# A sliding-window attention with a gated layer behind it: one written list gives the order of every engine

## The chip, the core and the metric

The kernel runs on one core of one Trainium2 chip. The metric is the device time of one execution in microseconds (us), taken as the median of several runs. The engines are TensorE (PE, with its weight loads PEld), VectorE (DVE), ScalarE (ACT), GpSimd (POOL) and SyncE (SP). SP, ACT and POOL can issue DMA transfers.

## The reference

There are 8 batches of 8 heads with 576 positions and 64 columns. The attention sees the last 128 positions only and has a linear bias for each head; its result, 4608 tokens of 512 columns, goes through two matrices with a gate between them.

```
scores = q @ k.T / sqrt(64) + slope[head] * -|i - j|      # where 0 <= i - j < 128, else -1e9
attn   = softmax(scores);  x = (attn @ v), heads side by side: [4608, 512]
h = x @ w_in                      # [4608, 2048]
g = h * sigmoid(beta * h)
out = g @ w_out                   # [4608, 512]
```

Inputs and outputs are fp32; the kernel works in bf16 with sums in fp32.

## The kernel before

**Attention.** Tokens of a batch are taken in blocks of 128 (the fifth has 64). q, k and v are loaded in fp32 (`get`, `get_pair`, L200 to L222; tile `fst`, 14 buffers) by SP, cast to bf16 (`cast_qk`, `cast_pair`, `cast_v`, tile `bst`, 4 buffers, or straight into `VS`), and q and k are turned so that the 64 columns lie on partitions (`QK`). For batches 0 and 1 a step `TP` does this on PE, one pair of heads at a time, with one copy by DVE for k and one by ACT for q (L289, L293); for later batches a transposing DMA of SP does it (`DT`, L409). From batch 3 on, v comes by a casting DMA that POOL issues (`get_v`).

Scores of two heads come into two PSUM banks, computed by matmuls on 64 rows, two at a time (`SP_` for batches 0 and 1, in a part A and a part B; `SC`, L438, for the others, m = 0 or 1). ACT takes exp of them (tile `pt`), DVE multiplies by the decay and mask (`factor`, L171 and L176), PE multiplies by v with a column of ones (`PVP`, `PV`, `PVB`), DVE divides by the sum (`norm`, L358 and L359, L499 and L500), and the result is turned into `XT` (features on partitions, a ring of 1536 tokens): on PE with a copy for batches up to 3 (`XP`, `X`), by a transposing DMA of SP later. The last 64 rows of batches 0 and 1 go their own way (`TT`, `SCT`, `PV`).

**The gated layer.** Nine groups of 512 tokens. For each group 16 hidden tiles (`Hm`, L557: four matmuls of 512 columns, then tanh by ACT into `sig`, L564, then one DVE operation into `gT`, L565, which makes h * (1 + tanh(beta h / 2))) and four output tiles (`OS`, L588: 16 matmuls in four steps, then a copy with the factor 0.5 by ACT into `osb`, L598, 5 buffers, then a store). `W1` and `W2` come in four pieces of 512 KB each (in bf16) by casting DMAs that POOL issues.

**Order.** PE, SP and POOL run in the order in which the program calls the steps (a manual schedule); for the first steps ACT and DVE do so too, later a scheduler places them. The calls are made by hand for the first 16 hidden tiles and by a spreading function afterwards (`spread`): it lays the attention steps of later batches (`att`) between hidden and output steps in proportion to their weights. In one call, a step does its matmuls and also the work of ACT and DVE on them. PSUM is handed out by pools (`psum_t`, `psum_h`, `psum_x`, later `psum_o` and `psum_s`) with names for their uses: `SS`, `ST` and `SX` for scores, `hps`, `hpo`, `ops` and `oph` for hidden and output tiles. The last output tile is made in two column halves of 256, which share a bank (L588 to L599).

Dummy matmuls on zeros (`idle`, `calm`) keep PE busy while it waits at the start.

Of the kernel before, what the change touches and what calls it, by code (L numbers as in the profile page):

```python
# [15 lines left out]
P = 128  # L16


@with_exitstack
def kernel(  # L20
# [18 lines left out]
    NQB = 5  # L39
# [44 lines left out]
    psum_c = ctx.enter_context(tc.tile_pool(name="psum_c", bufs=1, space=bass.MemoryType.PSUM))  # L84
    psum_h = ctx.enter_context(tc.tile_pool(name="psum_h", bufs=2, space=bass.MemoryType.PSUM))
    trans = ExitStack()
    psum_t = trans.enter_context(tc.tile_pool(side="right", name="psum_t", bufs=2, space=bass.MemoryType.PSUM))
    SS = psum_c.tile([P, 2, 512], F32, name="SS")
    psum_c.seal()
    opening = ExitStack()  # L90
    psum_x = opening.enter_context(tc.tile_pool(name="psum_x", bufs=1, space=bass.MemoryType.PSUM))
    SX = psum_x.tile([P, 2, 512], F32, name="SX")
    late, gates = {"tick": 0}, {}
    spans = [SS]

    def span():

        spans.append(spans.pop(0))
        return spans[-1]

    def obank(name, tag=None):
        if tag is None:
            late["n"] = late.get("n", 0) + 1
            tag = "ops" if late["n"] % 2 else "h3"
        return late["o"].tile([P, DM], F32, name=name, tag=tag)[:]

    def after(ins, other):
        tc.add_manual_dep(
            ins.ins, other.ins.name,
            mybir.DependencyInfo(mybir.DependencyClass.Sync, mybir.DependencyReason.DATA),  # L110
            reason="gate",
        )

    def idle(n):
        for _ in range(n):
            nc.tensor.matmul(
                SS[:, 0, :], lhsT=zeros[:, 0:P], rhs=zeros[:], start=True, stop=True,
                skip_group_check=True)  # L120

    def constants():
# [4 lines left out]
        idle(8)  # L127
# [35 lines left out]
    def falls_late(i):  # L163
        to, a, w = ((0, 0, P), (128, 0, 64), (192, 0, P), (320, 1, 64), (384, 1, P))[i]
        after(nc.vector.tensor_copy(
            out=falls[:, :, to : to + w], in_=fall[:, :, a, 0:w]), gates[1, 4])

    def factor(pt, m, p):

        if m:  # L170
            nc.vector.tensor_tensor(  # L171
                out=pt[:], in0=pt[:], in1=falls[:, 2 * p : 2 * p + 2], op=ALU.mult)
            return
# [16 lines left out]
    def betas():  # L190
        bps = psum_t.tile([P, NFF], F32, name="bps", tag="t")
        nc.tensor.transpose(out=bps[:], in_=bflat[:], identity=identf[:])
        nc.vector.tensor_scalar_mul(beta_h[:], bps[:], 0.5)
# [7 lines left out]
    def get(what, b, sb):  # L201
# [5 lines left out]
        return nc.sync.dma_start(  # L207
# [4 lines left out]
    def get_pair(b, p):  # L212

        r = []
        for what, src in (("k", k), ("q", q)):
            f = fst_pool.tile([P, 2, 4, D], F32, name="fst", tag="fst")
            fs[what, b, "p", p] = f
            r.append(nc.sync.dma_start(  # L218
                out=f[:].rearrange("r h c d -> r h (c d)"),
                in_=src[b, 2 * p : 2 * p + 2, 0:FULL, :].rearrange("h (r c) d -> r h (c d)", c=4),  # L220
            ))
        return r[0]  # L222

    def cast_qk(b, sb):
        rows = ROWS[sb]
        t = bst_pool.tile([P, 2, H, D], BF16, name="bst", tag="bst")
        staged[b, sb] = t
        nc.gpsimd.tensor_copy(out=t[0:rows, 0], in_=fs.pop(("q", b, sb))[0:rows])  # L228
        return nc.gpsimd.tensor_copy(out=t[0:rows, 1], in_=fs.pop(("k", b, sb))[0:rows])  # L229

    def cast_pair(b, p):
# [663 lines left out]
```

The softmax here doesn't subtract the row's maximum and nothing guards it: scores larger than these inputs give would overflow.

## Time and profile before

| what | value |
|---|---|
| runs of the kernel | 325.4, 325.74, 326.25 us; median 325.74 |
| span of the profiled execution | 324.0 us (first to last instruction; the time of that execution itself is not given beside it) |
| PE busy | 312.7 us, 97% of the span |
| ACT busy | 194.1 us, 60% |
| DVE busy | 183.1 us, 57% |
| POOL busy | 98.8 us, 30% |
| hidden and output matmuls, 512 columns | 216 ns from one start to the next when nothing holds them |
| TensorE clock granted | 0.999 of full |

The profile's page lists busy time by engine, then the span in 40 slices (a digit is the busy share of a slice in tenths), the DMA queues, the chain of waits that ended last, and the costliest groups of instructions. The windows view gives busy time by stretch. In the timeline a row has start, length, engine, line, operation, the tile written and the tile read, a count, and in brackets the idle time of the engine ahead of it and what ended it. A busy PE is not PE at its peak, since records of pipelined matmuls overlap.

### The profile page before, as it was taken

The page shows a single profiled execution, that of the slowest core. Times are in us where ns is not written, and L with a number is a line of the kernel's source. Part 1 is how long each engine was busy: PE and PEld are TensorE (multiplying, and loading weights), DVE is VectorE, ACT ScalarE, POOL GpSimd, SP SyncE. Part 2 cuts the span into 40 slices and gives each one's busy share as a digit, 9 for nine tenths or more (in the row PEclk, how much of TensorE's full clock was granted, in tenths as well). Part 3 has the DMA queues.
Part 4 walks back from the last instruction along what each step waited for, and adds up shares of the span by engine and source line. Part 5 has one row for each costly group of instructions (what it writes and reads, how often), then busy time and mean ns, then how long its engine had stood idle before and what let it go on. Part 6 is the DMA issues. An engine that isn't in the chain of part 4 may idle for free.

```text
span 324.0 us, 5988 instructions
## 1 busy us (share of the span) xinstructions
PE 312.7 (97%) x2297; PEld 153.3 (47%) x2297; DVE 183.1 (57%) x346; ACT 194.1 (60%) x283; POOL 98.8 (30%) x154
## 2 busy tenths in 40 slices
PE   8888999999999999999999999999999999999995
PEld 3454554443545454544454545444544455444443
DVE  5777877542548753785178717752775176335500
ACT  6857887635558865685467635845675465346511
POOL 4864820333873455356226232340000000000000
PEclk9999999999999999999999999999999999999999
DMA  7999999998999999999969994993222112110021
GB/s 221 252 263 238 176 196 196 215 199 162 214 181 208 222 208 139 230 217 148 257 153 196 150 245 94 211 138 107 18 65 60 65 18 65 46 62 32 10 90 65
DMA packets 147565, 48.84 MB, mean 151 GB/s; under 512 B 135360, under 2 KB 143824, under 8 KB 147536
## 3 DMA queue, kind: packets, MB, share of 16 engines
q1 hardware_dynamic: 115712, 32.39, 56.1%
q0 software_dynamic: 28624, 10.29, 26.1%
q10 hardware_dynamic: 3200, 5.78, 5.1%
q8 instruction: 18, 0.29, 0.4%
q14 instruction: 11, 0.09, 0.1%
HBM read 36.71 MB, written 9.44 MB: 142 GB/s over the span
## 4 chain that ended last, share of the span: by engine, by line
PE 69%; DMA 17%; SPq 6%; POOL 2%; ACT 2%; DVE 2%; issue 1%; POOLq 0%; DVEq 0%
PE ops L588 21%; PE hps L557 21%; PE hpo L557 10%; PE oph L588 7%; DMA fst<-in_v_dram 6%; DMA qkT<-bst 6%; SPq L207 3%; DMA fst<-in_q_dram 3%; DMA fst<-in_k_dram 2%; PE SS L438 2%; SPq L218 2%; PE ST L438 1%; PE SS L495 1%; PE SS L492 1%; POOL bst L229 1%
## 5 line engine op out<-in xcount | busy, mean ns | idle before, releaser
L588 PE MATMUL ops<-W,gT 128*128 128x512 bf16 (+1 forms) x464 | 109.7, 372 | 0.5 <-ACT osb L598 0.5
L565 DVE SCALAR_TENSOR_TENSOR gT<-sig,hps 128x512 bf16<-128x512 bf16 x100 | 67.6, 683 | 71.8 <-ACT sig L564 71.5
L557 PE MATMUL hps<-XT,W 128*128 128x512 bf16 x400 | 99.9, 379 | 0.3 <-DVE XT L533 0.3
L564 ACT ACTIVATE sig<-hps,beta_h 128x512 bf16<-128x512 f32 x100 | 68.1, 690 | 34.6 <-PE hps L557 33.2
L588 PEld LDWEIGHTS <-gT 128*128 128x128 bf16 x592 | 55.7, 98 | 61.6 <-issue 1.9
L557 PEld LDWEIGHTS <-W 128*128 128x128 bf16 x576 | 52.9, 98 | 60.8 <-issue 3.6
L228 POOL CAST bst<-fst 128x512 bf16<-128x512 f32 (+1 forms) x32 | 20.8, 650 | 74.4 <-DMA fst<-in_q_dram 42.4
L557 PE MATMUL hpo<-XT,W 128*128 128x512 bf16 x168 | 43.1, 379 | 0.0
L564 ACT ACTIVATE sig<-hpo,beta_h 128x512 bf16<-128x512 f32 x42 | 29.0, 690 | 16.9 <-PE hpo L557 16.9
L565 DVE SCALAR_TENSOR_TENSOR gT<-sig,hpo 128x512 bf16<-128x512 bf16 x42 | 28.6, 681 | 11.2 <-ACT sig L564 11.0
L598 ACT ACTIVATE osb<-ops 128x512 f32<-128x512 f32 (+1 forms) x28 | 16.6, 595 | 25.5 <-PE ops L588 25.5
L446 ACT ACTIVATE pt<-SS 128x1024 bf16<-128x1024 f32 x24 | 24.5, 1020 | 11.6 <-PE SS L438 11.1
L588 PE MATMUL oph<-W,gT 128*128 128x512 bf16 x128 | 29.3, 379 | 0.0
L229 POOL CAST bst<-fst 128x512 bf16<-128x512 f32 (+1 forms) x32 | 22.1, 690 | 15.6 <-DMA fst<-in_k_dram 15.0
L176 DVE TENSOR_TENSOR pt<-pt,fall 128x1024 bf16<-128x1024 bf16 x24 | 17.1, 712 | 14.8 <-ACT pt L446 14.8
L446 ACT ACTIVATE pt<-ST 128x1024 bf16<-128x1024 f32 x24 | 24.5, 1022 | 0.0
L171 DVE TENSOR_TENSOR pt<-pt,falls 128x1024 bf16<-128x1024 bf16 x24 | 18.8, 791 | 9.3 <-ACT pt L446 9.3
L250 POOL DMA_DIRECT2D vs<-in_v_dram x25 | 21.3, 869 | 0.2 <-issue 0.2
L598 ACT ACTIVATE osb<-oph 128x512 f32<-128x512 f32 x8 | 4.8, 597 | 21.1 <-PE oph L588 21.1
L495 PEld LDWEIGHTS <-pt 128*128 128x128 bf16 x240 | 14.8, 97 | 4.2
L243 POOL CAST vs<-fst 128x512 bf16<-128x512 f32 (+1 forms) x15 | 10.5, 703 | 15.9 <-DMA fst<-in_v_dram 15.9
L438 PEld LDWEIGHTS <-qkT 64*128 64x128 bf16 x240 | 8.9, 94 | 12.5 <-issue 12.0
(102 smaller groups left out, 257.8 us busy)
## 6 DMA issues: line engine op xcount, KB each, us to landing
fst<-in_k_dram SPq DMA_DIRECT2D x32, 256.0 KB, 6.0
fst<-in_q_dram SPq DMA_DIRECT2D x32, 256.0 KB, 5.3
out_dram<-osb ACTq DMA_DIRECT2D x22, 256.0 KB, 2.0
fst<-in_v_dram SPq DMA_DIRECT2D x12, 256.0 KB, 5.4
out_dram<-osb POOLq DMA_DIRECT2D x12, 256.0 KB, 5.2
vs<-in_v_dram POOLq DMA_DIRECT2D x20, 128.0 KB, 6.1
W<-in_moe_w_in_dram POOLq DMA_DIRECT2D x4, 512.0 KB, 7.9
W<-in_moe_w_out_dram POOLq DMA_DIRECT2D x4, 512.0 KB, 12.8
```

The costliest lines, as they stand in the source:

```text
L171: nc.vector.tensor_tensor(out=pt[:], in0=pt[:], in1=falls[:, 2 * p : 2 * p + 2], op=ALU.mult)
L228: nc.gpsimd.tensor_copy(out=t[0:rows, 0], in_=fs.pop(("q", b, sb))[0:rows])
L229: return nc.gpsimd.tensor_copy(out=t[0:rows, 1], in_=fs.pop(("k", b, sb))[0:rows])
L250: return nc.gpsimd.dma_start(out=VS[b % 2][0:rows, sb, :, 0:D], in_=v[b, :, P * sb : P * sb + rows, :].rearrange("h p d -> p h d"))
L438: nc.tensor.matmul(o, lhsT=qk[64 * e : 64 * e + 64, 1, p, P * kb : P * kb + P], rhs=qk[64 * e : 64 * e + 64, 0, p, P * kb : P * kb + nq], ...
L446: nc.scalar.activation(out=pt[:], in_=sps[:], func=ACTF.Exp, scale=qscale)
L495: nc.tensor.matmul(o, lhsT=weights(b, qb, h, 0), rhs=vs[:, qb, h, 0 : D + 1], start=qb == 0, stop=True, skip_group_check=True)
L557: nc.tensor.matmul(hps, lhsT=W1[:, c, bass.ts(j, P)], rhs=XT[:, c, c0 : c0 + TOKG], start=(c == 0), stop=(c == NDM - 1),)
L564: gates[g, j] = nc.scalar.activation(out=sig[:], in_=hps, func=ACTF.Tanh, scale=beta_h[:, j : j + 1])
L565: gates["gT"] = nc.vector.scalar_tensor_tensor(out=gts[g][:, j, :], in0=sig[:], scalar=1.0, in1=hps, op0=ALU.add, op1=ALU.mult)
L588: nc.tensor.matmul(ops_[:, cols], lhsT=gT[:, j, i * P : i * P + P], rhs=W2[:, j, cols], start=(j == 0), stop=(j == NFF - 1),)
L598: nc.scalar.mul(o, ops_[:, cols], 0.5)
```

## The change

Every step is cut into its parts by engine: `TP` now only transposes and `TPC` copies; `SP_` only makes scores and `EP` takes exp; `Hm` is followed by `HA` (tanh) and `HD` (the DVE operation); `OS` by `OC` (the copy, with the engine named) and `store` (with the engine named). A text, `PLAN`, of some 1300 such steps is read from front to back, and each step is issued where it stands. All five engines run in that order. A step's name carries the engine where there is a choice (`.p` POOL, `.v` DVE, `.a` ACT, `.s` SP); numbers are batch, part, pair or block, and for PE steps the bank.

PSUM is one tile of eight banks, and each step names its own. Casts are spread over POOL, ACT and DVE; copies of `TP` and `XP`, and the output copies, take ACT or DVE as named. The order of loads, of the weights' pieces, of hidden tiles (no more in rising order), of output steps and of stores is another. The loads of q, k and v into `fst` are issued by SP, as before, and v of batches 3 to 7 and the weights by POOL, as before. The plan was drawn up for at most eight transfers in flight at a time; no instruction enforces it beyond the semaphores that both programs have. The gate that held back `falls_late` and the first transposing DMA is gone. The last output tile is made in two halves in two banks (`OL`).

```diff
+PLAN = """
+const q.s:0:2 k.s:0:0 fr:0 order q.s:0:0 q.s:0:1 ck.v:0:0 cq.a:0:0 Rk:0:0:4 beta:1 q.s:1:0 k.s:0:3
+Rq:0:0:2 z:2:0 k.s:0:1 k.s:0:2 q.s:0:3 cq.v:1:0 rq.a:0:0 cq.p:0:1 rk.v:0:0 gv.s:0:1 B:0:0:5:0
+A:0:0:0:1 gv.s:0:2 ck.a:0:3 gv.s:0:3 cq.p:0:2 ck.v:0:2 fr:5 EB:0:0 gv.s:0:0 Rq:0:2:5 k.s:1:1 k.s:1:0
+Rk:0:2:3 EA:0:0 cv.p:0:2 Rk:0:3:4 rq.v:0:2 rk.a:0:2 w1:0 q.s:1:1 w1:1 z:2:2 Rq:0:1:5 fr:4 MB:0:0
+fr:6 fr:2 rq.a:0:1 q.s:1:2 cq.a:0:3 ck.a:0:1 A:0:2:6:1 rk.v:0:3 B:0:2:2:1 w1:2 cv.p:0:3 cv.p:0:0
+ck.p:1:0 z:1:0 Rk:0:1:1 ck.p:1:1 k.s:1:3 Rq:0:3:5 rk.v:0:1 ones EB:0:2 EA:0:2 z:1:3 rq.v:0:3
+B:0:1:3:0 EB:0:1 A:0:3:1:1 cv.v:0:1 MB:0:1 A:0:1:5:1 Rq:1:0:0 EA:0:3 k.s:1:2 VB:0:1:3 rq.v:1:0 z:2:4
+VB:0:2:2 EA:0:1 nB:0:1 nB:0:2 VA:0:3:4 VA:0:2:0 VA:0:1:7 Rk:1:0:3 nA:0:3 rk.a:1:0 cq.a:1:1 B:0:3:5:1
+VB:0:0:1 EB:0:3 nA:0:2 nA:0:1 gv.s:1:3 VA:0:0:2 A:1:0:3:1 VB:0:3:7 XP:0:2:6 q.s:1:3 cq.p:1:2 nA:0:0
+gv.s:1:1 ck.p:1:2 gv.s:0:4 gv.s:1:0 nB:0:0 EA:1:0 gk.s:0:4 XP:0:0:0 nB:0:3 xc.v:0:0 xc.a:0:2
+Rk:1:1:3 XP:0:1:5 gq.s:0:4 ck.a:1:3 Rq:1:2:2 XP:0:3:4 fr:7 fr:3 Rq:1:1:1 Rk:1:3:0 xc.a:0:1 rk.a:1:1
+h:0:1:7:0:3 xc.a:0:3 h:0:0:3:0:3 h:0:0:3:3:4 rq.a:1:1 cq.p:1:3 rq.a:1:2 a:0:0 d:0:0
...
+O:7:3:3:1 OL:1:7 O:8:1:1:2 oc.a:7:1 O:8:2:1:4 O:8:2:2:4 O:8:1:2:2 O:8:1:3:2 oc.v:7:2 oc.v:7:3 lc.a:1
+st.s:7:0 st.s:7:1 st.p:7:2 ls.s:1 oc.a:8:0 O:8:2:3:4 st.p:7:3 oc.a:8:2 st.a:8:2 oc.v:8:1 st.p:8:0
+st.s:8:1 OL:0:5 lc.a:0 ls.a:0
+"""
...
+    PS = psum.tile([P, 8, 512], F32, name="PS")
+    def bank(k):
+        return PS[:, k, :]
+    def move(eng, out, in_):
+        (nc.scalar.copy if eng is nc.scalar else eng.tensor_copy)(out=out, in_=in_)
...
+    def cast_qk(what, eng, b, sb):
...
+        move(eng, staged[b, sb][0:rows, "qk".index(what)], fs.pop((what, b, sb))[0:rows])
...
+    def TPC(what, eng, b, p):
+        tps = held.pop((what, b, p))
...
+    def EP(vis, b, p):
...
+        nc.scalar.activation(out=pt[:, :, 0:w], in_=sps[:, :, 0:w], func=ACTF.Exp, scale=qscale)
...
+    def HA(g, j):
+        hps = hs[g, j]
+        sig = held["H", g, j] = sig_pool.tile([P, TOKG], BF16, name="sig", tag="sig")
+        nc.scalar.activation(out=sig[:], in_=hps, func=ACTF.Tanh, scale=beta_h[:, j : j + 1])
...
+    def OL(part, bk):
+        g, i, gT = NTG - 1, 3, gts[NTG - 1]
+        late[g, i, part] = bank(bk)
+        cols = slice(256 * part, 256 * part + 256)
+        for j in range(NFF):
+            nc.tensor.matmul(
+                late[g, i, part][:, cols], lhsT=gT[:, j, i * P : i * P + P], rhs=W2[:, j, cols],
+                start=(j == 0), stop=(j == NFF - 1),
+            )
...
+    with tc.manual_schedule(engines={ENG.PE, ENG.SP, ENG.Pool, ENG.Activation, ENG.DVE}):
+        for step in PLAN.split():
+            name, *at = step.split(":")
+            name, _, eng = name.partition(".")
+            STEPS[name](*([ENGINES[eng]] if eng else []), *map(int, at))
```

Names used below: `Rk` and `Rq` transpose k and q of a pair on PE, `rk` and `rq` copy them out; `ck`, `cq`, `cv` (and `cK`, `cQ`) cast; `k`, `q`, `gk`, `gq`, `gv` load; `A` and `B` are scores of batches 0 and 1, `EA` and `EB` their exp; `VA` and `VB` the products with v, `nA` and `nB` their division, `XP` and `xc` the turn into `XT`; `S`, `E`, `M`, `V`, `n`, `X`, `x` the same for later batches, `D` and `XD` the transposing DMAs; `H` or `h`, `a`, `d` a hidden tile, its tanh and its DVE operation; `O`, `oc`, `st` an output step, its copy and its store; `z` dummy matmuls.

## The prediction

> **What bounds the kernel now.** I read the page first (busy shares, slices), then the windows, then the timeline of the first 25 us and of the end, then the waits. TensorE (PE) is busy 97% of the span at the full clock, so only gaps between its matmuls can be won.
>
> ```profile
> PE 312.7 (97%) x2297; PEld 153.3 (47%) x2297; DVE 183.1 (57%) x346; ACT 194.1 (60%) x283; POOL 98.8 (30%) x154
> PEclk9999999999999999999999999999999999999999
> DMA  7999999998999999999969994993222112110021
> ```
>
> The reader is to see that ACT, DVE and POOL have 40% to 70% of room on average, that the clock is never the limit after the start, and that the DMA engines are full for the first 60% of the span.
>
> Busy time flatters PE, because pipelined matmuls overlap in the records. So I added up the matmuls that start in each stretch at the pace at which the timeline shows them unhindered: 216 ns for 512 columns, 162 for 384, 109 for 256, 56 for 128, 29 for 65, and half of that for the 64-row score matmuls, which run in pairs. The sum is 294.5 us. The first matmul starts at 1.2 and the last ends at 320.5, so 26 us are not work: 5.2 in 0-10, 3.2 in 10-20, 1.9 in 20-30, 2.3 in 30-40, 2.0 in 40-50, 3.6 in 50-100, 4.5 in 100-180, 3.4 after. More than half lies in the first 50 us, where ACT and DVE are busiest:
>
> ```profile
> 0.00:10.00 10.00, 7.93 (x48) 3.60 (x49) 6.72 (x28) 7.12 (x15) 5.19 (x16) 1.00 0.84 233
> 10.00:20.00 10.00, 8.90 (x124) 5.03 (x124) 7.04 (x21) 7.21 (x11) 8.81 (x15) 1.00 1.19 272
> 30.00:40.00 10.00, 9.19 (x99) 4.68 (x100) 7.83 (x18) 7.87 (x12) 8.84 (x15) 1.00 1.02 188
> 100.00:180.00 80.00, 79.23 (x610) 39.06 (x609) 52.13 (x89) 54.24 (x78) 37.28 (x53) 1.00 1.29 198
> ```
>
> (Columns: PE, PEld, DVE, ACT, POOL busy, clock, DMA.) In the timeline of the start, loads arrive about 1.2 us apart and each releases a cast:
>
> ```profile
> 2.61 2.54 ACT L142 ACTIVATE fallq<-relq 128x256 bf16<-128x256 f32 x8
> 3.60 1.35 POOL L235 CAST bst<-fst 128x512 bf16<-128x512 f32 x2 [1.71 <-DMA fst<-in_k_dram]
> 5.82 0.61 POOL L235 CAST bst<-fst 128x512 bf16<-128x512 f32 x1 [0.86 <-DMA fst<-in_k_dram]
> 7.10 0.61 POOL L235 CAST bst<-fst 128x512 bf16<-128x512 f32 x1 [0.66 <-DMA fst<-in_q_dram]
> 8.23 0.61 POOL L243 CAST vs<-fst 128x512 bf16<-128x512 f32 x1 [0.51 <-DMA fst<-in_v_dram]
> ```
>
> Eight activations of 402 ns each take 2.54 us together, so neighbours on ACT overlap by 85 to 120 ns: 1.02 counts as 0.93 in a dense queue, 0.69 as 0.57. After 50 us the losses are of two kinds: 24 score visits (L438), each with some 0.28 lost on entering and leaving the 64-row matmuls, 6.7 us; and single stalls of 0.23 to 0.76 us (at 74.1, 91.7, 96.1, 103.7, 122.3, 172.0 and 317.9), 3.6 us together. The last is the two column halves of the last tile in one bank:
>
> ```profile
> 318.20 0.38 ACT L598 ACTIVATE osb<-ops 128x256 f32<-128x256 f32 x1 [1.15 <-PE ops L588]
> 318.64 1.91 PE L588 MATMUL ops<-W,gT 128*128 128x256 bf16 x16 [0.47 <-ACT osb L598]
> ```
>
> **What the Trainium skill says.** "TensorE: Matmul & The Clock Gate", Part 1: half clock at first, then columns / 2.4 GHz + 2.5 ns. The trace agrees: the first dummies start 427 ns apart, later ones 216. "DMA: Bandwidth & Descriptors", Queues, rings and completion order: each DMA engine takes turns between queues by packet. The trace agrees: with a weight load on POOL's queue, SP's 256 KB loads landed up to 14 us after issue, against some 5 without. Two prices for casts from fp32: "ScalarE: Activation LUTs", What ACT_TABLE_LOAD costs, gives 186 + 0.833 N ns, so 0.61 for 512; its nearest trace row, XT<-xtp, has 0.59. "VectorE: DVE Perf Modes", The perf-mode tier table, has fp32 copies in SBUF at two elements a cycle; with the 150 cycles that page gives as fixed, I estimate 0.42 (the trace's 128-wide relb cast, 0.22, fits).
>
> **The change, part by part.**
> *Same work.* Both programs have the same matmuls, 16 dummies and all, so PE work stays 294.5. Of 95 casts on POOL 50 leave: 24 go to ACT (24 x 0.6 = 14 us) and 26 to DVE (26 x 0.42 = 11); nine output copies go from ACT to DVE (9 x 0.69 = 6). POOL drops by 50 x 0.65 = 32 us. After 50 us this hides: ACT and DVE were busy 68% of a stretch at most.
> *The first 26 us.* SP issues another batch-0 load (q.s:0:2) ahead of the first pair, and q.s:1:0 as the fifth. On DVE the cast cq.v:1:0 stands ahead of rk.v:0:0, the copy of the first keys; the fifth load landed at 8.2 in the trace, so the first scores can't start before 9.2 (6.6 now). On ACT ck.a:0:3 (sixth load, 8.9) stands ahead of the first exp, which thus starts at 9.6 (7.0 now). From there to xc.a:0:3, the copy that lets group 0 finish its hidden matmuls, ACT has 4 EB x 0.93 + 5 EA x 0.73 + 4 key or query copies and 3 XT copies x 0.5 + 4 casts x 0.52 = 13 us: 22.6 if it never waits. But ck.a:1:3 stands in that queue. Its load is the 18th on SP, and w1:0 to w1:2 are now issued by POOL one after the other at about 14 to 17 us. Loads 14 to 18 are pairs; next to a weight load the trace has a pair landing 1.73 us after the one before (20.80 to 22.53) or 3.15 (14.63 to 17.78). I take 1.73, the middle of the trace's next three (2.3, 0.7, 1.7): with load 14 at 16.7, 16.7 + 4 x 1.73 = 23.6. Then cast, two copies, copy: group 0 goes on at 25.8. PE has 12.9 us of work behind it by then: 12.9 lost. Now that point is reached at 22.1: 9.2 lost.
> *26 to 53 us.* Now another 5.7 are lost until 36.3 us of work are done (at 51.2). In the new order the batch-1 scores and hidden tiles alternate more finely. ACT's queue from there to a:0:12 is 23.7 us by single durations, about 20.3 overlapped; PE's is 24.3, so PE leads again. Lost: five 64-row visits x 0.28 = 1.4, and I allow 1.0 for banks whose evacuation is just late (H:0:10 and SCT:0 among them). Sum 15.3, against 14.9 now: **+0.4**.
> *After 53 us.* I measured, along the new PE order, the work between the last matmul in a bank and its next use, and between producer and consumer (hidden tile to its output matmul, score to V, V to X). Nearly all exceed the evacuation times from the page's groups (0.69 + 0.68 for a hidden tile, 1.02 for an exp, 0.9 for a norm) with over 0.3 to spare. So the 3.6 us of single stalls go, that of the last tile too (OL uses banks 7 and 5). 25 score visits instead of 24 cost 0.3 more. **-3.3.** SP's queue carries loads, transposes and now 13 more stores; a store waits for its copy, and the loads and transposes behind it wait too. That they are at most eight in flight is no new limit: in the trace each SP load already waits for the one eight before it. The batch-2 transposes should land by 72 us and are needed at 76, which covers this; without that cover each late us costs one.
> *The end* stays: copy and store after the last matmul, 3.5 us.
>
> Sum -2.9: span 324.0 to 321.1. The page doesn't give the profiled run's own time; the three runs, 325.4 to 326.25, lie 1.4 to 2.3 above its span, and I carry the difference to the median: 325.74 to **322.8**.
> Bounds of what no row shows: casts on ACT or DVE at 0.4 to 0.7 instead move the start by 2 x 0.2 at most; the fine interleaving may win the 1.0 allowed or cost 3; the 3.6 may stay whole or go; the loads are the large one (below).
>
> **Rivals.**
> (a) *The start is faster too.* If loads land before the weight traffic bites, ACT never waits and group 0 goes on at 22.6: 3.2 less, 319.6; with no late banks, 318.6. For it: pairs land 0.8 us apart when alone. Against: POOL issues three weight loads with nothing between.
> (b) *Slower: the queue behind a late load.* At 3.15 us a pair the 18th load lands at 29.3, and ACT, in order, holds the copies behind ck.a:1:3: 5.7 more, **328.5**. It decides from a landing at 27.5 on (326.7). For it: v loads took 14 us there. Against: those have 256-byte pieces, pairs 1 KB.
> (c) *Nothing gained.* The single stalls after 50 us come back at other places, as every engine now waits in one fixed order and DMA times vary: 326.1, within what is measured as no change.
>
> **How the numbers follow.** Main case 45%, its own range 320.5 to 324.7; (a) 18%, (b) 25%, (c) 12%. A measurement of this kernel can tell about 0.3%, 1 us, from no change. Main case and (a) give 0.63 for faster; (c) 0.12 for the same, (b) 0.25 for slower. The range reaches from (a) with some more, 317.0, to (b), 328.8.
>
> **What would show it.** Right: first EB or EA exp at 9 to 10 us; first tanh of group 0 at about 27 (22.3 now); PE without gaps over 0.3 us after 53; the last two 256-column groups back to back. Wrong: ACT waiting for a load in 20 to 30 us for over 4 us (b), or hidden tiles of group 0 complete before 24 (a); score matmuls waiting for qkT transposes at 70 to 100 us would break the late gain.

## The result, and the profile after

The kernel after takes 328.24 us (median of 12 runs, 324.97 to 332.73), the kernel before 325.35 beside it (12 runs, 324.6 to 326.25). The ratio is 1.0061, 95% interval 1.0037 to 1.0085: slower by 0.6%, where 322.8 us was forecast. Ratios with intervals leave out the longest runs of each kernel; medians and ranges here are of all runs. Beside each other the kernel after spreads over 8 us and the kernel before over 2; beside the later experiments before spread over 2.9 to 6.3 us, in 18 to 58 runs.

The profiled execution took 328.33 us, its span is 326.5. From its page (busy time of the engines; then, by slices of the span, the granted clock and the share of the DMA engines):

```profile
PE 311.2 (95%) x2297; PEld 154.2 (47%) x2297; DVE 196.3 (60%) x385; ACT 195.0 (60%) x294; POOL 66.7 (20%) x104
PEclk9799999999999999999999999999999999999999
DMA  7999999999999999999989989771469003200223
```

PE does the same work with more idle time. POOL fell by 32.1 us, as forecast; DVE rose by 13.2 and ACT by 0.9, where the prediction's counts come to 17 and 8. The clock has a dip in the second slice, and the DMA engines are full through slice 20 and little less to slice 25. The windows (busy us of PE, PEld, DVE, ACT, POOL; clock; DMA share; GB/s), the same stretches as of before and then one more:

```profile
0.00:10.00 10.00, 6.44 (x29) 2.26 (x31) 5.19 (x24) 6.44 (x14) 2.30 (x11) 0.93 0.81 250
10.00:20.00 10.00, 9.43 (x111) 5.34 (x110) 7.52 (x21) 7.54 (x12) 6.55 (x9) 0.90 1.22 258
30.00:40.00 10.00, 9.13 (x82) 4.49 (x82) 8.34 (x16) 9.91 (x15) 4.09 (x6) 1.00 1.12 179
100.00:180.00 80.00, 79.02 (x613) 39.20 (x611) 54.84 (x98) 54.73 (x80) 22.36 (x31) 1.00 1.34 197
60.00:90.00 30.00, 26.02 (x167) 12.31 (x166) 17.30 (x34) 15.23 (x21) 7.01 (x10) 1.00 1.19 197
```

The last stretch, in the kernel before:

```profile
60.00:90.00 30.00, 29.73 (x222) 14.21 (x221) 12.98 (x24) 15.65 (x22) 13.35 (x21) 1.00 1.15 200
```

From 60 to 90 us PE is busy 3.7 us less, while the DMA engines move as much: 197 against 200 GB/s. By the same sum of matmuls at their own pace as in the prediction, the loss when so much PE work is done:

| PE work done, us | 12.9 | 36.3 | 55 | 75 | 100 | 180 | 250 | last matmul ends |
|---|---|---|---|---|---|---|---|---|
| lost in before | 9.2 | 14.9 | 15.6 | 17.4 | 19.6 | 23.4 | 25.2 | 320.5 |
| lost in after | 10.7 | 14.6 | 14.6 | 19.8 | 21.0 | 26.7 | 28.5 | 323.2 |

Up to 55 us of work the kernel after leads by 1.0. From there to 75 us of work (69.6 to 94.8 us of its span) it loses 3.4 us against before, and 0.9 more up to 250; the last 45 us of work give 0.6 back. The waits of PE from 60 to 200 us (us in total, times, longest):

```profile
PE PS L523 <- DMA qkT<-bst: 2.9, 2, 1.7
PE PS L633 <- DMA XT<-xn: 1.5, 2, 0.7
PE PS L656 <- DMA W<-in_moe_w_out_dram: 1.1, 1, 1.1
PE PS L523 <- DVE gT L646: 0.4, 1, 0.4
PE PS L633 <- ACT XT L206: 0.2, 1, 0.2
```

5.5 of 6.1 us end with a DMA: scores wait for batch 2's transposes, hidden tiles for transposes of `XT`, an output step for W2's last quarter (`w2:3` in the plan). The timeline has the first three of these waits, and on POOL and SP's queue what went before them:

```profile
65.10 0.62 POOL L206 CAST bst<-fst 128x512 bf16<-128x512 f32 x1 [3.84 <-DMA fst<-in_q_dram]
65.66 0.74 POOL L355 DMA_DIRECT2D W<-in_moe_w_out_dram  x1
67.24 8.94 SPq L501 DMA_TRANSPOSE qkT<-bst  x3
74.43 3.61 PE L656 MATMUL PS<-W,gT 128*128 128x512 bf16 x16 [1.11 <-DMA W<-in_moe_w_out_dram]
79.24 0.83 PE L523 MATMUL PS<-qkT 64*128 64x256 bf16 x12 [1.20 <-DMA qkT<-bst]
84.66 0.61 PE L523 MATMUL PS<-qkT 64*128 64x256 bf16 x9 [1.67 <-DMA qkT<-bst]
```

POOL issues w2:3 only at 65.7, since it stands in its list behind a cast that waited 3.84 us for a load. The quarter lands at 74.4; batch 2's transposes, beside that traffic, at 70.0, 76.0, 78.4, 79.2 and 84.6 (68.3 to 80.0 in before, where all of W2 had landed by 55.2).

The end came out as forecast. The last 256-column half follows at once (no idle time in brackets, where before had 0.47).

```profile
321.28 1.91 PE L667 MATMUL PS<-W,gT 128*128 128x256 bf16 x16
```

### The profile page after: what moved, and what is told of

Same layout as the page of the kernel before. It is cut to its first block, busy times and chain, and to the rows that moved or that the text cites. A ratio compares the mean times of both kernels' runs of the same rounds, so it can differ in the third digit from the quotient of the medians.

```text
span 326.5 us, 5978 instructions
## 1 busy us (share of the span) xinstructions
PE 311.2 (95%) x2297; PEld 154.2 (47%) x2297; DVE 196.3 (60%) x385; ACT 195.0 (60%) x294; POOL 66.7 (20%) x104
## 2 busy tenths in 40 slices
DMA packets 147565, 48.84 MB, mean 150 GB/s; under 512 B 135360, under 2 KB 143824, under 8 KB 147536
## 4 chain that ended last, share of the span: by engine, by line
PE 73%; DMA 14%; SPq 4%; ACT 3%; DVE 2%; issue 1%; POOL 0%; ACTq 0%; POOLq 0%
PE PS L656 31%; PE PS L633 31%; DMA fst<-in_q_dram 6%; PE PS L523 4%; DMA qkT<-bst 3%; DMA fst<-in_v_dram 2%; PE PS L578 2%; SPq L307 2%; DMA out_dram<-osb 2%; DVE gT L646 2%; PE PS L575 2%; SPq L501 1%; DMA XT<-xn 1%; ACT sig L641 1%; PE PS L667 1%
## 5 line engine op out<-in xcount | busy, mean ns | idle before, releaser
L633 PE MATMUL PS<-XT,W 128*128 128x512 bf16 x576 | 135.9, 379 | 1.7 <-DMA XT<-xn 1.5
L656 PE MATMUL PS<-W,gT 128*128 128x512 bf16 x560 | 133.7, 379 | 1.1 <-DMA W<-in_moe_w_out_dram 1.1
L641 ACT ACTIVATE sig<-PS,beta_h 128x512 bf16<-128x512 f32 x144 | 93.9, 691 | 65.0 <-PE PS L633 60.5
L646 DVE SCALAR_TENSOR_TENSOR gT<-sig,PS 128x512 bf16<-128x512 bf16 x144 | 93.7, 683 | 61.9 <-ACT sig L641 61.6
L532 ACT ACTIVATE pt<-PS 128x1024 bf16<-128x1024 f32 x48 | 47.2, 1025 | 13.1 <-PE PS L523 13.0
L206 POOL CAST bst<-fst 128x512 bf16<-128x512 f32 (+1 forms) x35 | 23.6, 687 | 115.8 <-DMA fst<-in_k_dram 41.8
L678 ACT ACTIVATE osb<-PS 128x512 f32<-128x512 f32 (+1 forms) x27 | 15.5, 582 | 33.2 <-PE PS L656 12.5
L587 DVE TENSOR_TENSOR xn<-PS,zb 128x512 bf16<-128x512 f32 (+1 forms) x30 | 20.7, 690 | 1.0
L523 PE MATMUL PS<-qkT 64*128 64x256 bf16 (+2 forms) x240 | 15.2, 250 | 3.3 <-DMA qkT<-bst 2.9
L578 PE MATMUL PS<-vs,pt 128*128 128x65 bf16 x240 | 17.2, 193 | 0.0
L523 PEld LDWEIGHTS <-qkT 64*128 64x128 bf16 x240 | 9.0, 94 | 12.9 <-issue 9.6
```

Of the source, the lines that this page charges most:

```text
L206: (nc.scalar.copy if eng is nc.scalar else eng.tensor_copy)(out=out, in_=in_)
L523: nc.tensor.matmul(o, lhsT=qk[64 * e : 64 * e + 64, 1, p, P * kb : P * kb + P], rhs=qk[64 * e : 64 * e + 64, 0, p, P * kb : P * kb + nq], ...
L532: nc.scalar.activation(out=pt[:], in_=held.pop(("S", b, m, p)), func=ACTF.Exp, scale=qscale)
L578: nc.tensor.matmul(o, lhsT=weights(b, qb, h, 0), rhs=vs[:, qb, h, 0 : D + 1], start=qb == 0, stop=True, skip_group_check=True)
L587: nc.vector.tensor_tensor(out=xn[0:nq].rearrange("p (g h) d -> p g h d", g=2), in0=pv[0:nq, :, :, 0:D], in1=zs[0:nq].broadcast_to([nq, 2, ...
L633: nc.tensor.matmul(hps, lhsT=W1[:, c, bass.ts(j, P)], rhs=XT[:, c, c0 : c0 + TOKG], start=(c == 0), stop=(c == NDM - 1),)
```

## Experiments

Six theories are tested. Theory 1: w2:3, issued late, is late itself and its traffic delays batch 2's transposes. Theory 2: loads of batches 3 and 4 stand ahead of those transposes on SP's queue. Theory 3: the fixed order on ACT and DVE costs time as such. Three came later. Theory 4: the time goes in the narrow stretch before 55 us. Theory 5: the DMA engines are full, so that a step moved ahead makes another one late. Theory 6: casts on DVE and ACT stop these engines at a late load.

Some traces lack about 40 of some 2300 matmul records (3% of PE's work), so runs are compared by the tanh instructions, which are all there: T1 is the start of the last tanh of group 1; T2 runs from there to the first of group 2 (the stretch of the three stalls); T3 from there to the end of the last matmul. PE's work in each is the same in all kernels made from after. T1 to T3 come from one execution of each kernel. The last column has the median of the kernel before, run beside it.

| run | T1 | T2 | T3 | median us (range, runs) | ratio to before, 95% | before |
|---|---|---|---|---|---|---|
| after | 69.4 | 28.8 | 225.0 | 328.2 (325.0-332.7, 12) | 1.0061 [1.0037, 1.0085] | 325.4 |
| r_after_again | 71.2 | 28.6 | 222.9 | 328.7 (326.5-331.8, 6) | 1.0095 [1.0058, 1.0132] | 325.2 |
| e1_w2_early | 71.8 | 25.4 | 225.4 | 327.5 (324.5-331.0, 20) | 1.0042 [1.0016, 1.0067] | 325.1 |
| e2_loads_behind | 69.6 | 27.6 | 225.2 | 329.5 (327.4-332.2, 4) | 1.0156 [1.0080, 1.0231] | 325.1 |
| e3_both | 75.5 | 25.0 | 224.2 | 329.1 (326.7-330.2, 4) | 1.0105 [1.0056, 1.0155] | 325.1 |
| e6_xt_first | 70.5 | 27.8 | 226.2 | 327.5 (325.8-329.5, 7) | 1.0077 [1.0049, 1.0105] | 325.2 |
| e8_w1_later | 73.1 | 24.4 | 226.8 | 329.0 (327.4-330.9, 6) | 1.0112 [1.0074, 1.0150] | 325.2 |
| e9_all | 70.6 | 25.2 | 222.7 | 328.7 (323.8-334.6, 14) | 1.0041 [1.0006, 1.0076] | 325.2 |
| e9b_all_again | 74.7 | 25.9 | 223.6 | 329.5 (1) | | 325.6 |
| e10_w1_behind_k | 73.6 | 25.3 | 223.6 | 327.5 (325.0-333.0, 22) | 1.0045 [1.0018, 1.0071] | 325.6 |
| e12_half_bytes | 70.4 | 24.4 | 221.9 | 321.5 (320.9-325.7, 6) | 0.9871 [0.9817, 0.9926] | 325.6 |
| e14_no_w1_move | 70.0 | 27.7 | 223.1 | 329.5 (325.8-334.4, 22) | 1.0083 [1.0056, 1.0110] | 325.9 |
| e15_small_later | 69.2 | 28.2 | 226.9 | 328.6 (325.0-333.7, 21) | 1.0050 [1.0024, 1.0076] | 325.9 |
| e16_need_order | 72.7 | 24.8 | 225.8 | 328.5 (326.0-330.6, 11) | 1.0082 [1.0049, 1.0114] | 326.2 |
| e17_need_small | 69.5 | 25.3 | 227.6 | 328.4 (325.7-332.8, 11) | 1.0065 [1.0034, 1.0096] | 326.2 |
| e18_need_small_dummies | 70.8 | 25.1 | 226.6 | 328.3 (325.2-329.9, 20) | 1.0059 [1.0037, 1.0081] | 326.2 |
| e19_casts_on_pool | 69.6 | 26.6 | 224.1 | 326.5 (324.9-329.9, 13) | 1.0050 [1.0021, 1.0079] | 324.8 |

Two kernels are made from before: e5_before_w2_late, 327.12 (325.8-328.8, 11), ratio 1.0058 [1.0037, 1.0080]; e13_before_half_bytes, 324.85 (323.9-325.9, 22), ratio 0.9967 [0.9949, 0.9986].

But for e12 the interval of every kernel made from after overlaps that of after. So a difference of about a microsecond between their medians is not shown, and what the reorderings do is read from their stages.

**The three stalls: e1, e2, e3.** e1 moves one step:

```diff
-cK.a:2:2 w2:2 d:1:10 ... cQ.p:2:2 w2:3 a:1:14
+cK.a:2:2 w2:2 w2:3 d:1:10 ... cQ.p:2:2 a:1:14
```

> The kernel after with one step moved: the last quarter of W2 is issued by POOL right behind the third quarter, at about 46 us where it was 65.7. Theory 1 (the late weight quarter is late itself and its traffic holds up batch 2's transposes): the stalls at 73.1, 77.7 and 82.8 us (1.28, 1.36 and 1.83 us) all nearly go, batch 2's transposes land by 76 us, and the time falls by about 4 us, to about 324. Theory 2 (loads of batches 3 and 4 that stand ahead on SyncE's queue make the transposes late, whatever W2 does): only the stall at 73.1 goes, the other two stay within 0.5 us of their size, and the time falls by 1 to 1.5 us. Theory 3 (the fixed order on ScalarE and VectorE as such): no change beyond 0.5 us.

Measured: T2 fell by 3.4 us. The wait for W2 is gone; PE's wait for the transposes from 60 to 97 us is

```profile
PE PS L523 <- DMA qkT<-bst: 1.8, 2, 1.3
```

against 2.9: they landed at 73.1 to 83.7. The second of these transposing DMAs took SP 1.6 us to issue; in after, beside the quarter, it took 5.1. So the size was nearly Theory 1's for the stretch, but two of the stalls only shrank, and the median is 0.7 lower (against before beside it, 0.5), not 4. r_after_again, below, has much the same T1 and a T2 of 28.6, so the gain in T2 is the edit's and not a late start's. e2 moves seven loads and two casts:

```diff
-gq.s:4:4 ... gq.s:3:2 ... gk.s:3:2 ... gq.s:3:0 ... gq.s:3:4 ... cQ.p:3:4 ... cK.v:3:2 ... gk.s:3:1 gq.s:3:1 D:2:3
+D:2:3 gq.s:4:4 gq.s:3:2 gk.s:3:2 gq.s:3:0 gq.s:3:4 gk.s:3:1 gq.s:3:1 cQ.p:3:4 cK.v:3:2
```

> The kernel after with seven loads of batches 3 and 4 (and two casts that need them) moved behind batch 2's last needed transpose on SyncE's list; the weight quarter stays where it was. Theory 1: the transposes still meet the weight quarter's traffic (66 to 74 us), the stalls at 77.7 and 82.8 us lose at most a third, and the time falls by 0 to 1 us. Theory 2: seven loads at about 1.15 us each are out of the way, the transposes land 5 to 7 us earlier, both stalls go, and the time falls by about 3 us, to about 325; the stall of 1.28 us at 73.1 stays. Theory 3: no change beyond 0.5 us.

Measured: the transposes landed at 64.1 to 73.9, up to 11 us earlier and in time: Theory 2's landing. The wait for W2 went too, which Theory 2 didn't have: the cast ahead of w2:3 got its load earlier, so POOL issued the quarter at 61.9 instead of 65.7. But T2 fell by 1.2 only, since two new waits stand further on in the timeline:

```profile
87.70 0.43 PE L578 MATMUL PS<-vs,pt 128*128 128x65 bf16 x8 [1.07 <-DVE vs L206]
95.27 0.39 PE L523 MATMUL PS<-qkT 64*128 64x256 bf16 x4 [1.56 <-DMA qkT<-bst]
```

Batch 2's values and batch 3's transposes are late now. The stall was moved. e3 is both edits.

> Both edits together. Theory 1: as with the weight quarter alone, about 324. Theory 2 and any mixture of the two: all three stalls go, about 4.5 us less, 323.5 to 324. If the time stays above 326, the three stalls are not what the kernel loses, and something later takes the time back.

Measured: no wait for a DMA from 73 to 85 us and T2 at 25.0, yet 329.05. Its time went earlier, in instructions that it shares with after: T1 is 75.5 instead of 69.4. (That PE came 6 us later to the stretch can be all the reason why nothing was late there: e8, below, has as short a T2 by coming late alone.)

**The mirror in before: e5.**

```diff
-        w2 += [load_w2(n) for n in range(2, 4)]
+        w2 += [load_w2(n) for n in range(2, 3)]
...
-                    r.append(lambda sb=sb: (cast_qk(b, sb - 2), DT(b, sb - 2)))
+                    r.append(lambda sb=sb: (cast_qk(b, sb - 2), sb == 3 and w2.append(load_w2(3)), DT(b, sb - 2)))
...
-            after(r, w2[3])
+            after(r, w2[-1])
```

> The kernel before with the last quarter of W2 issued late: by POOL behind the casts of batch 2's second 128 rows, at about 65 us instead of 39, and batch 2's first transpose gated by the third quarter instead of the fourth. Theory 1: the same harm appears here, batch 2's transposes land 3 to 5 us later than 68 to 77 us, and the time rises by 2 to 4 us, to about 328. Theory 2: the transposes have no loads of later batches ahead of them, they still land in time for the scores at 76 us, and only the output step that needs the quarter waits, 0 to 1.5 us more.

Measured: 2.0 us slower. POOL issued the quarter at 62.3, and the waits from 60 to 80 us are

```profile
PE ops L588 <- DMA W<-in_moe_w_out_dram: 1.2, 1, 1.2
PE SS L438 <- DMA qkT<-bst: 0.6, 1, 0.6
```

The second was 0.27 in before; the transposes landed at most 1.6 us later. The late quarter costs its own wait, and in before it hardly touches the transposes. The size is Theory 1's, the place of the harm Theory 2's.

**Does the early loss repeat: r_after_again, e8, e9, e9b, e10, e6.** First the kernel after once more, with no edit.

> The kernel after once more, unchanged, to see which of its stalls come back and which are one execution's. If the loss between 55 and 90 us and the spread of 2 per cent have one fixed cause (theories 1 and 2), the stalls at 73, 78 and 83 us come back within 0.5 us each, and the first 55 us repeat within 1 us. Theory 4 (weight loads of POOL's queue overtake or do not overtake small loads of SyncE's queue, by a margin smaller than the jitter of the start): stalls between 25 and 55 us come and go by 2 to 6 us from one execution to the next.

Measured: the waits for the transposes at 79 and 84 come back, 3.3 us together (2.9 in after), that for W2 with 0.5. Seven profiles begin with the same instructions up to 41.8 us (after, this one, e1, e2, e3, e6, e14), and their T1 runs from 69.4 to 75.5. In e3, the longest, 1.9 us of the 6.1 are there at the first tanh. Two rows of the timeline and one of the windows (PE, clock, DMA share, GB/s) go with the rest:

```profile
42.18 0.40 PE L386 MATMUL PS<-ident,bst 64*128 64x64 bf16 x8 [1.72 <-DVE bst L206]
44.57 2.08 PE L454 MATMUL PS<-vs,pt 128*128 128x65 bf16 x35 [1.25 <-POOL vs L206]
44.00:48.00 4.00, 3.10 (x53) 0.50 1.01 159
```

The two waits come to 3.0 us, where after has one of 1.6 in this stretch. From the end of the first on, the granted clock was half (42.8 to 49.6 us), and matmuls of 512 columns started 427 ns apart instead of 216; in after it was full there. So a stall can cost more than its own length.

The first wait is for the cast of q's last 64 rows, whose load landed at 41.6 (35.5 in after). In after SP issued the k and q loads of these rows at 29.6 and 31.5, both ahead of w1:3 (31.8 on POOL), and they took 5.3 and 4.0 us to land. In e3 they went out at 30.9 and 34.2, with w1:3 between them at 33.0, and took 9.8 and 7.5. e8 moves w1:3 out of that stretch:

```diff
-h:0:1:7:3:4 w1:3 gk.s:1:4 ... cv.p:1:2 a:0:8
+h:0:1:7:3:4 gk.s:1:4 ... cv.p:1:2 w1:3 a:0:8
```

> The kernel after with one step moved: the last quarter of W1 is issued by POOL behind the cast of batch 1's third block of values (about 41 us) instead of ahead of it (31 to 34 us), so that its traffic can't stand beside the 64-row loads of batch 0 and that block's load. Theory 4: the stall at 38.9 us (1.72 us) and the larger ones seen in some executions (up to 6 us between 37 and 48 us) go, the median falls by 2 to 3 us and the spread of the runs from 8 us to under 4. Theories 1 and 2: at most 1.7 us less, the spread stays.

Measured: 329.0, no gain. The waits for the small loads went and W1 was late in their place:

```profile
45.80 1.24 PE L633 MATMUL PS<-XT,W 128*128 128x512 bf16 x4 [3.28 <-DMA W<-in_moe_w_in_dram]
```

(Here too the clock was half behind the stall, from 46.5 to 49.9.) But T2 fell to 24.4 with no edit there: PE arrived 3.7 us later, and the transposes had landed. What a stage loses ahead is given back where the DMA sets the pace. e6 moves five loads behind `XD`:

```diff
-XD:4:1 gk.s:5:4 gq.s:7:2 XD:4:0 ... gq.s:7:1 gq.s:6:4 D:6:0 ... gq.s:7:3 XD:4:4 XD:5:0 ... XD:5:1 D:6:3
+XD:4:1 XD:4:0 gk.s:5:4 gq.s:7:2 ... D:6:0 ... XD:4:4 XD:5:0 ... XD:5:1 gq.s:7:1 gq.s:6:4 gq.s:7:3 D:6:3
```

> The kernel after with five loads of batches 5 to 7 moved on SyncE's list from ahead of the transposes of normalised rows (batch 4 block 0; batch 5 blocks 0 and 1) to behind them. If those loads hold the transposes up, the waits of the hidden-layer matmuls at 154 and 188 us (0.9 each, up to 1.6) go and the time falls by 1.5 to 2.5 us; if the transposes are late because their rows are normalised late, nothing changes.

Measured: both waits for `XT` gone, a new one of 3.3 us at 193 (`PE PS L523 <- DVE gT L646` in the waits), 327.5. e9 has the edits of e1, e2, e6, e8 and two swaps at the start (rk.v:0:0 ahead of cq.v:1:0, ck.a:0:3 behind EB:0:0).

> The kernel after with all moves at once: last quarter of W2 early, seven loads behind batch 2's transposes, last quarter of W1 later, XT transposes ahead of five loads, and at the start the copy of batch 0's first k ahead of a cast for batch 1 on VectorE and the fourth k cast behind the first exponential on ScalarE. If stalls only add up: 4.5 + 1.7 + 2 + 1 us less than after, about 319 to 320, below the kernel before. If the program waits for the same bytes whatever their order, 324 to 326.

Measured: its profiled execution took 323.77, the fastest run of any kernel made from after that carries all its bytes; its 14 runs reach 334.6, median 328.7. A second profile of it, e9b, was taken on another chip:

> All moves at once, a second look, unchanged from the kernel of that name: its profiled execution was 323.8 us, the median of its runs 328.7. Theory 4: a slow execution loses its time before 55 us, in waits for loads that stand beside W1's last quarter, and the late part (75 us of PE work to the end) repeats within 1.5 us. If the spread came from everywhere, the late part would differ by as much as the early part.

Measured: T1 4.1 us longer (its wait for W1 at 47 is 3.1 us, for 1.3 in the first profile, and the clock was half from 48.5 to 51.9 behind it), T2 and T3 longer by 0.7 and 0.9. So between these two executions most of the difference comes from before 75 us, as Theory 4 says. e10 issues w1:3 earlier than e8, has the edits of e1, e2 and e6, and moves gv.s:2:4 behind gq.s:2:3. It also has e9's two swaps at the start, although its expectation says that the start is as in after:

```diff
-h:0:1:7:3:4 w1:3 gk.s:1:4 ... cK.p:0:4 a:0:7
+h:0:1:7:3:4 gk.s:1:4 ... cK.p:0:4 w1:3 a:0:7
```

> All moves at once but two: W1's last quarter is issued by POOL behind the cast of batch 0's last 64 rows of k (so that it can't stand beside that load, but some 3 us earlier than behind the value cast), the start of VectorE and ScalarE is as in the kernel after, and one load of batch 2's values moves behind batch 2's last q load. Theory 4: no wait of over 2 us between 36 and 48 us, median 323 to 325, spread under 5 us. If the DMA queues as a whole are the limit there, W1's quarter is late instead (1 to 3 us at 42 to 46 us), median 326 to 328.

Measured: 327.5 with a range of 8 us, the second answer: a wait of 2.1 us for W1 at 46 with the clock at half behind it, and one of 1.0 for a value cast at 37.

**Are the DMA engines the limit: e12, e13.** e12, from after (its casts, too, read four heads twice):

```diff
+        n = 4 if what != "v" and b >= 2 else H
         return eng.dma_start(
-            out=f[0:rows],
-            in_=src[b, :, P * sb : P * sb + rows, :].rearrange("h p d -> p h d"),
+            out=f[0:rows, 0:n], in_=src[b, 0:n, P * sb : P * sb + rows, :].rearrange("h p d -> p h d"))
```

> The kernel after with the loads of q and k of batches 2 to 7 halved: only four of the eight heads are read, and the cast writes them to both halves, so that every instruction is there as before and the DMA engines carry half the packets of these loads; the output is that of other inputs. Theory 5 (the DMA engines are full until about 150 us, so that a step moved ahead on the list makes another late): the stalls from 73 to 85 and at 154 and 188 us go, 5 to 7 us less than after, 321 to 323. Theory 3 (the fixed order on the engines): under 1 us less.

Measured: 321.54, 6.7 less than after (6.9 if each median is set against before beside it, 6.2 by the two ratios): Theory 5's answer. No wait for a DMA is left from 60 to 200 us. The casts took as long as in after (medians of 0.42 us on DVE and 0.61 on ACT), so it is the bytes that count. The DMA share is still high to slice 22 but now has gaps, with 41.76 MB moved for 48.84:

```profile
DMA  6999999799999699999499859541658012200223
DMA packets 119917, 41.76 MB, mean 131 GB/s; under 512 B 107712, under 2 KB 116176, under 8 KB 119888
```

e13 makes the same cut in before (the load, and the two casts of `cast_qk`).

> The kernel before with the same cut: the loads of q and k of batches 2 to 7 read four of the eight heads and the casts write them to both halves; the output is that of other inputs. In the kernel after the cut was worth 6.7 us (328.2 to 321.5). Theory 5 with order as the difference (before's transposes come in time although the DMA engines are full): 0.5 to 2 us less here, 323 to 324.5. If before is held by the DMA engines as much as after: 4 us or more less, below 321.

Measured: 324.85, 1.0 less than before beside it: the first answer. Under the same full engines before loses one us to the bytes that were cut, after over 6; with these bytes gone after is the faster by 3.0 us (each set against before beside it). So the fixed order costs nothing as such, against Theory 3: it costs where loads are late. Counted in the traces, the transfers landed by a time are as many, but other ones (loads of q and k / of v / transposes of q and k):

| landed by | before | after |
|---|---|---|
| 75 us | 58 (36 / 10 / 3) | 57 (34 / 13 / 1) |
| 105 us | 84 (42 / 19 / 10) | 82 (47 / 16 / 8) |
| 150 us | 123 (60 / 25 / 19) | 125 (64 / 27 / 16) |

This fits the Trainium skill, "DMA: Bandwidth & Descriptors", Issuing engines are not separate DMA queues: whoever issues a transfer, it runs on the same 16 engines beside the others.

**A list by need: e14 to e19.** e14 is e1, e2 and e6 alone, the first 46 us as in after.

> The moves behind 46 us alone: W2's last quarter early, seven loads behind batch 2's transposes, the transposes of normalised rows ahead of five loads; the first 46 us are those of the kernel after. Theory 4 and 5 together: the late part as with all moves (some 4 us less than after), the waits for W1 of 1.3 to 3.4 us at 42 to 45 us gone, median 323 to 325, at or below the kernel before. If the order is a sum of zero under full DMA engines: 326 to 328.

Measured: 329.5, neither answer. Its profile loses as little as before up to 70 us of work (15.9), then come the waits of e2 again: 0.78 for values and

```profile
95.83 0.40 PE L523 MATMUL PS<-qkT 64*128 64x256 bf16 x4 [2.31 <-DMA qkT<-bst]
```

e15 also moves gv.s:2:4 behind gq.s:2:3 and gq.s:2:4, gk.s:2:2 behind gk.s:2:3.

> As the kernel with the moves behind 46 us alone, and three loads of batch 2 (last rows of v and q, third block of k), which stand at 33 to 39 us among the loads of batches 0 and 1, moved behind batch 2's first loads. Theory 4: 2.5 us less traffic in the narrow stretch, the waits between 38 and 44 us (1.1 to 1.7 us, up to 3.4 in some executions) fall below 0.7 us, and the median is 1 to 2 us below that kernel's. If the stretch is set by the start's jitter: within 0.5 us of it.

Measured: no wait over 0.3 us from 38 to 44 in its profile, T1 the shortest of all (69.2), the median 0.9 lower; the range stays. T3 is long, 226.9: behind stalls of 2.0 us at 93 and 2.3 at 192 the clock was half for 3.4 us each time. e16 is e1, the six loads of batch 3 of e2, and

```diff
-gq.s:4:2 ... gk.s:4:2 ... D:3:2 ... D:3:0 gk.s:3:3 D:3:1 st.s:0:3
+D:3:2 ... D:3:0 gk.s:3:3 D:3:1 gq.s:4:4 gq.s:4:2 gk.s:4:2 st.s:0:3
...
-XD:4:1 gk.s:5:4 gq.s:7:2 XD:4:0
+XD:4:1 XD:4:0 gk.s:5:4 gq.s:7:2
```

> The moves behind 46 us once more, with SyncE's loads in the order in which their batches are needed: W2's last quarter early, six loads of batch 3 behind batch 2's transposes, three loads of batch 4 behind batch 3's first three transposes (so far two of them stood ahead), and the transpose of batch 4's first normalised rows ahead of two loads. Theory 5: the waits of 0.9 and 2.5 us at 86 to 95 us that came with seven loads behind batch 2's transposes go, the late part loses under 12 us from 41.7 us of work to the end (13.7 in after, 10.9 in the kernel with the moves behind 46 us), median about 2 us below that kernel, 326 to 327.5. A sum of zero: new waits later, as much as those that went.

Measured: both waits at 86 to 95 gone, as Theory 5 had it, and a new one at 100, as the sum of zero had it. Its cause is another; in the timeline:

```profile
100.76 0.75 DVE L206 CAST bst<-fst 128x512 bf16<-128x512 f32 x1 [3.16 <-DMA fst<-in_q_dram]
101.43 1.26 DVE L646 SCALAR_TENSOR_TENSOR gT<-sig,PS 128x512 bf16<-128x512 bf16 x2
102.15 0.97 PE L523 MATMUL PS<-qkT 64*128 64x256 bf16 x12 [2.08 <-DVE gT L646]
```

DVE stands at a cast (cQ.v:3:3) whose load is late; the `gT` multiply that frees the bank is queued behind it, and PE waits for the bank. e17 is e16 with e15's three loads.

> The same, and the three small batch-2 loads out of the stretch before 41 us. Theory 4 and 5: the late part as there, the stretch from 25 to 42 us of work loses under 2.5 us, median 325 to 326. A sum of zero: as with the first alone.

Measured: T1 is 69.5 and T2 25.3, so the three stalls are gone with PE no later than in after; and it is 328.4 all the same. T3 is the longest of all. It has the DVE wait (2.4 us) in it, with the clock at half from 99.5 to 102.9, from its end on. e18 adds dummies to e17:

```diff
-Rq:0:0:2 z:2:0
+z:3:0 Rq:0:0:2 z:5:0
```

> The same, and six more dummy matmuls in TensorE's two gaps at 5 to 9 us (three ahead of the first q transposes, three more ahead of the first scores). If the low granted clock at 8 to 15 us costs time (kernels of this family with a mean clock under 0.99 took 1 to 3 us longer): clocks of 0.995 to 1.0, the median 1 to 2 us lower and the spread smaller than without. If the clock only follows the gaps and nothing waits for TensorE there: clocks up, time within 0.5 us.

Measured: the second answer. PE is busy from 5 to 8 us and the clock stays full at 8 to 15 (windows of PE: busy, clock, DMA share, GB/s):

```profile
5.00:8.00 3.00, 3.00 (x17) 1.00 1.02 338
8.00:10.00 2.00, 1.09 (x12) 1.00 1.04 328
10.00:12.00 2.00, 1.53 (x22) 1.00 1.25 229
```

In after those three rows have clocks of 1.00, 0.63 and 0.51. The mean clocks of the runs rise from 0.986 to 0.996, the median stays: 328.3 for 328.4. So the low clock of the start isn't what makes the median. (The range falls from 7.0 to 4.7 us, but before's beside them is 6.3.) e19, from e17, puts all casts of q and k of batches 2 to 7 on POOL, and batch 4's three loads behind gq.s:3:3:

```diff
-cK.a:2:4 cK.a:2:2 ... cK.v:2:1 ... cQ.v:3:3 ... cQ.a:4:2
+cK.p:2:4 cK.p:2:2 ... cK.p:2:1 ... cQ.p:3:3 ... cQ.p:4:2
```

> SyncE's list by need as in the last but one (with the three loads of batch 4 now behind batch 3's fourth q load), and all casts of q and k of batches 2 to 7 on POOL, as in the kernel before: 34 of 60 move there from VectorE and ScalarE, at the same places of the list. Theory 6 (a load that is late stops VectorE or ScalarE at its cast, and with it the multiplies and exponentials that free TensorE's banks; on POOL it stops only other casts and loads): the waits of 2 to 2.5 us at 97 to 100 us, and of 0.6 to 1 us at 193, go, the part from 75 us of work to the end loses under 6 us where the kernels with the moves lose 7 to 10, and the median falls 2 us below theirs, to 326 or less. If the DMA engines alone decide: 327.5 to 329, as those.

Measured: the waits at 97 to 100 and at 193 are gone, and the median is 2.0 us below e16's and e17's. But before was 1.4 lower beside it too; against before the gain is 0.5 us (1.7 above it, for 2.2), less than can be told apart. The part from 75 us of work on loses 9.2, not under 6: waits of 1.3 for a transpose at 93, and of 0.7 each for ACT and DVE at 133 to 137. Theory 6 has its waits right and its gain wrong. e19 moved casts and three loads at once, so the share of the casts isn't known. No version that carries all the bytes beat the kernel before.

## Why the prediction was wrong

*First 26 us: right in kind, too dear by 0.7 to 2.2 us.* Forecast: first exp at 9 to 10, group 0 on at 25.8, first tanh at about 27. The timeline has

```profile
8.67 0.61 PE L422 MATMUL PS<-qkT 64*128 64x128 bf16 x6 [1.37 <-DVE qkT L206]
9.32 1.02 ACT L432 ACTIVATE pt<-PS 128x1024 bf16<-128x1024 f32 x1 [0.56 <-PE PS L422]
```

with the reason that was given, the copy rk.v:0:0 behind a cast on DVE. Group 0's last hidden matmuls went on at 25.6 in after and 27.2 in r_after_again, first tanh at 26.0 and 27.6. But PE had 14.8 us of work behind it by then, not 12.9; at 12.9 us of work 10.7 and 12.2 were lost, for a forecast of 12.9 and 9.2 in before. Rival (b), ACT behind the 18th load, did not come: that load landed at 20.9 and 23.9, with 23.6 forecast. Nor did (a).

*26 to 53 us: right.* 15.3 lost was forecast at 36.3 us of work; 14.6 and 16.3 came. What this step lacked is the difference between executions: by T1, the same instructions come out up to 6 us apart.

*After 53 us: the step that failed.* Forecast was -3.3 us. From 36.3 us of work to the last matmul after lost 14.1 us and before 11.1, so it was +3.0. The step took all the single stalls of before away by an argument on banks: enough PE work lies between two uses of a bank. But three of those stalls, at 74.1, 96.1 and 172.0, ended with a transposing DMA, not with a bank that came free. The waits of before from 50 us on have

```profile
PE SS L438 <- DMA qkT<-bst: 1.3, 3, 0.5
```

and beside them 1.0 us that ended with DVE or ACT. The half on banks held: what ends with DVE or ACT fell to 0.6 us in after, 0.2 at 138 and 0.4 at 194. What ends with a DMA, which the step put at nothing, rose from 1.3 to 5.5 us. For it the prediction had one sentence, that batch 2's transposes "should land by 72 us and are needed at 76, which covers this". The cover did not hold: the last four of them landed at 76.0 to 84.6. The span came out 5.4 over the forecast (326.5 for 321.1). e12 comes near the step as it would have been with the cover: 321.5, with no wait for a DMA, 1.3 below the forecast (the cut also thins the traffic from 37 us on).

The line that broke this was named in the prediction ("each late us costs one"), but the 72 us has no working there; it lies among the landing times of the kernel before (68.3 to 80.0), which has another list. The prediction read from before's page that the DMA engines are full for the first 60% of the span. Then a landing time depends on all the bytes ahead of it on every queue, and that sum was not made for the new list. Loads of batches 3 and 4 ahead of batch 2's, landing some 1.15 us apart, and W2's quarter behind a cast were in the text of the plan to be counted. Nor is a late us always one: in the profiles of kernels made from after a stall of about 2 us or more was often followed by half clock (last section).

*Casts on DVE and ACT, "After 50 us this hides": in part.* 0.62 us on ACT and 0.42 on DVE, where POOL doesn't stand in the way, were right as durations. That a cast in a fixed order also carries its load's lateness to what is queued behind it was reckoned for ACT in the first 26 us, not for DVE after 53; e16 shows it at 2.1 us.

*The end: right.*

*A reading that the trace doesn't bear out.* "each SP load already waits for the one eight before it": SP's 34th load in before was held from 43.5 to 52.0, and the 26th had landed at 35.8. Nothing in the sum rests on it.

*Chances.* Slower had 0.25, all of it on rival (b), which was not the cause. That 328.2 lies close to (b)'s 328.5, and so within the range that (b) widened, is luck. Rival (c) came nearest to the mechanism, stalls that come back elsewhere as every engine waits in one fixed order and DMA times vary; it priced them as the stalls of before, and those that end with a DMA came to four times as much.

Open: what in the start makes the early stage differ between executions; how the protection of the kernel before divides into the order of its loads and its casts on POOL; and how much of the median and the spread is half clock behind stalls, since no run has the stalls without it.

## What to carry to other kernels

Before new work is given a landing time, ask what each stall of the old kernel waited for: an argument on banks says nothing of a stall that ends with a DMA. Where the DMA engines are full, as here for 60% of the span, sum the bytes ahead of a transfer on all queues for the new order, and don't carry a landing time over from the old one. Here a load moved ahead made another late, so a stall taken away showed as a stall further on; compare stages, and halve the bytes to see what lateness costs in all. In a fixed order a step that waits for a load holds up what is queued behind it (2.1 us in e16), so try it on an engine that nothing urgent stands behind; e19 took such waits away, though its gain in time isn't shown.

## What the hardware showed that was not expected

*A cast on DVE that begins while one runs on POOL takes longer.* As a rule it ended 0.27 to 0.29 us after POOL's. Of after:

```profile
6.57 1.17 POOL L206 CAST bst<-fst 128x512 bf16<-128x512 f32 x2 [4.66 <-DMA fst<-in_q_dram]
7.29 0.73 DVE L206 CAST bst<-fst 128x512 bf16<-128x512 f32 x1 [1.58 <-DMA fst<-in_q_dram]
9.79 0.43 DVE L206 CAST bst<-fst 128x512 bf16<-128x512 f32 x1 [1.18 <-DMA fst<-in_k_dram]
```

It took 0.73 beside POOL's and 0.43 alone; two casts of values that begin beside POOL's show 0.78 and 0.80, and one in r_after_again, beside three of POOL's in a row, 1.93. Where DVE was first (70.1 us), its cast took 0.43 and POOL's 0.87. "SBUF — State Buffer", Terms, in the Trainium skill has a reason, and these rows agree with it: the two share a pair of ports, which an instruction holds to its end while the other blocks. Spreading casts over both gains less than their durations say.

*Short gaps of PE can be followed by half clock, and the same kind of gap need not be.* In after, gaps of 0.98 and 1.37 us between 5.5 and 8.7 us went before half clock from 8.5 to 11.9; in r_after_again, gaps of 0.92 and 0.82 at the same places left it full. Later it was the same: of twelve stalls of about 2 us or more between 30 and 315 us, in the profiles of kernels made from after, seven ended within 1.2 us of the start of half clock for 3.4 us, which is up to 1.7 us of PE's work lost on top of the stall (e8, e9b, e10, e15 twice, e16, e17). The other five, one of 3.3 us in e6 among them, left the clock full. In before and in e12 and e13 no stall reached 2 us in that stretch, and the clock stayed full there.
